# Stage 1 of a three-stage attention kernel: where the first group's leftover keys are multiplied, and as how many products

## The chip, the cores and the metric

The kernel runs on one core of a Trainium2 chip. The metric is the device time of one execution in microseconds (us); less is better. Beside the timed runs there is one profiled execution, whose trace all rows below come from. Engines are named as the profile names them: PE is TensorE (its weight loads stand apart as PEld), DVE is VectorE, ACT is ScalarE, POOL is GpSimd, and SP is SyncE, which issues most DMA transfers.

## The reference

Three layers follow each other: attention with rotary positions over 4 batches, 8 heads, 576 positions and 64 values a head; a gated feed-forward layer that mixes positions; and an attention layer with four experts. Only the first is touched. Cut to it:

```
def _attn_ref(q, k, v):
    ...
    q_rot, k_rot = (rotate(q), rotate(k))
    scale = 1.0 / np.sqrt(D)
    scores = scale * np.matmul(q_rot, k_rot.transpose(0, 1, 3, 2))
    scores = scores - np.max(scores, axis=-1, keepdims=True)
    attn = np.exp(scores)
    attn = attn / (np.sum(attn, axis=-1, keepdims=True) + 1e-09)
    return np.matmul(attn, v).astype(np.float32)
```

## The kernel before

Stage 1 is the attention layer. Its work comes in 16 units: one unit is a pair of heads of one batch. A unit has nine blocks of 128 query rows. Blocks 0, 2, 4, 6 hold queries of the first head and blocks 1, 3, 5, 7 of the second, 128 queries each; block 8 holds the last 64 queries of both heads. For each block the kernel makes the scores against the 576 keys in a PSUM tile `ps_S` (there are two, used in turn), the maximum of each row (`nmax`, on VectorE), the exponential (`e`, on ScalarE, straight from PSUM), and then transposes of `e` on TensorE (`ps_t`, four transposes of 128 keys each), which ScalarE or VectorE copies to SBUF (`g`). With the transposed exponentials as moving operand and the values `v` as weights TensorE makes the output, 64 rows for each head, in one PSUM tile `ps_o` of which there is only one.

576 keys are four times 128 and 64 left over. The leftover 64 keys of the two heads of a pair of blocks are put side by side by VectorE (`gather`), transposed together on TensorE (`ps_l`) and copied by ScalarE to `tl0` (first group) or `tl1` (second). The key rows 0 to 63 of `tl0` belong to the first head, 64 to 127 to the second. The weights for the leftover keys are kept as 128 rows by 2 x 64 columns, with zeros where key rows and output head don't belong together.

The output is made in two groups: the first group is the queries of blocks 0 to 3 (256 columns), the second those of blocks 4 to 8 (320 columns). `av(second, part)` issues the products of a group, and `out(second)` evicts `ps_o` with ScalarE (`xt`) and stores it through SyncE's queue.

A product for one head writes 64 of the 128 rows of `ps_o`, so it uses 64 columns of the array; the products of the two heads follow each other in column halves. The trace shows a plain f32 product as two records, so four products of one call stand as x8.

The order of instructions is written out by hand. The loop runs over slots k, of which each unit has nine, x = 0 to 8. Within slot x of a unit ScalarE makes the exponential of block x, TensorE the scores of block x + 1 (in slot 8: block 0 of the next unit) and the transposes of block x - 1, and VectorE the maximum of block x + 1. Around this regular work the other steps stand at given slots. For the unit whose slots these are, `av(False, 0)` stands at the end of slot 5, `av(False, 1)` at the end of slot 7 and `out(False)` in slot 8, behind the exponential. The second group follows in slots 1, 3 and 4 of the next unit (`av(True, 0)`, `av(True, 1)`, `out(True)`). Engines run their own instructions in this order; SyncE's queue is ordered by the recording layer.

Other work of stage 1 on the same engines: rotation of the next units' q and k on POOL and DVE, splitting of the weights `w_in` (`wt`, `raw`, `wih`; in most slots of odd units, in one of even units), and normalization of finished heads (`sa` times `sr`).

Of the kernel before, what the change touches and what calls it, by code (L numbers as in the profile page):

```python
# [40 lines left out]
def fused_kernel(ctx, tc, qk, v, w_in, w_out, w_sg, g_ln, b_sg, wqk, wvg, wo, rope, cst, out):  # L41
# [17 lines left out]
    PE, ACT, DVE, POOL = Engine(nc.tensor), Engine(nc.scalar), Engine(nc.vector), Engine(nc.gpsimd)  # L59
# [9 lines left out]
    def bank(t):  # L69
        shape = [P, 2, 512] if t.isupper() else [P, 512]  # L70
        return ps[t].tile(shape, F32, tag="b", name="ps_" + t)
# [271 lines left out]
    with ExitStack() as st:  # L343
# [19 lines left out]
        tl0 = ptp.tile([P, 256], F32, name="tl0")  # L363
# [10 lines left out]
        class Work:  # L374
# [110 lines left out]
            def av(self, second, part):  # L485


                if part == 0:
                    self.o = bank("o")
                n = 320 if second else 256  # L490
                for kb in ((0, 1), (2, 3, 4))[part]:
                    for j in range(2):
                        if kb < 4:
                            m = (g1 if second else g0)[:, kb, n * j:n * j + n]
                        else:
                            m = tl1[:, 64 * j:64 * j + 320] if second else tl0
                        PE.matmul(self.o[64 * j:64 * j + 64, 0:n], self.vt[:, kb, j, :], m, start=(kb == 0), stop=(kb == 4))
# [23 lines left out]
        def slot(k):  # L521


            n, x = divmod(k, 9)
            (nk, xk), (nn, xn) = divmod(k - 1, 9), divmod(k + 1, 9)
            w, p, wk, wn, nx = [works.get(i) for i in (n, n - 1, nk, nn, n + 1)]

            if w:
                w.exps(x)
            if x == 8 and w:  # L530
                w.out(False)
            if x == 4 and p:
                p.out(True)

            if wn:
                if xn == 0:
                    wn.start()
                wn.scores(xn)
            if wk:
                wk.turn(xk)  # L540
            for at, g, i in ((4, w, 0), (5, w, 1), (7, w, 2), (0, p, 3), (1, p, 4)):
                if x == at and g:
                    g.turn_left(i)
            if x == 1 and p:
                p.turn_factor()

            if wn:
                wn.maxima(xn)
            for at, g, i in ((1, w, 0), (3, w, 1), (5, w, 2), (7, w, 3), (0, p, 4)):
                if x == at and g:  # L550
                    g.gather(i)
            if x == 0 and p:
                p.factor(0)

            if n == 0 and x == 3:
                works[1].rope(1, (2,), DVE)
            if wk:
                wk.place(xk)
            if x == 0 and p:
                p.factor(1)  # L560
            if x == 2 and p:
                p.place_left(True)
                p.store_factor()
            if x == 5 and w:
                w.place_left(False)

            if x in (1, 3) and p:
                p.av(True, x // 2)
            if x in (5, 7) and w:
                w.av(False, x // 2 - 2)  # L570

            if nx:
                if x == (2 if n == 0 else 1):
                    nx.parts(0)
                if x == (4 if n == 0 else 3):
                    nx.parts(1)
                if n + 2 < B * NP:
                    if x == 3:
                        works[n + 2] = Work()
                        works[n + 2].load(n + 2)  # L580
                    if x == (7 if n == 0 else 4):
                        works[n + 2].rope(0)
                    if x == (8 if n == 0 else 7):
                        works[n + 2].rope(1)
                if x == 4 and n + 2 < B * NP:
                    works[n + 2].load_values()
# [30 lines left out]
        for k in range(9 * B * NP + 7):  # L617
            n, x = divmod(k, 9)
            slot(k)
            if x in ((1, 3, 4, 6, 7, 8) if n % 2 else (7,)):  # L620
                next(wload, None)
            if k == 9 * 4:
                steps = attended(bx, 0)
            if k == 9 * 14:
                lsteps = leftover(bx, 0)
            if n >= 4 and x == 8:
                next(steps, None)
            if n >= 14 and x == 3:
                next(lsteps, None)
            if k == 9 * 15 + 1:  # L630
                nsteps = attended(bx, 1)
            if k > 9 * 15 and x in (1, 5):
                next(nsteps, None)
# [37 lines left out]
    with ExitStack() as st:  # L671
# [210 lines left out]
        for b in range(1, B):  # L882
# [7 lines left out]
            if b == 2:  # L890
                w = wc.tile([P, 12, DM], F32R, tag="w", name="w")
# [28 lines left out]
    with ExitStack() as st:  # L920
# [436 lines left out]
        w, g = works[2 * B - 1], op[B - 1]  # L1357
# [102 lines left out]
```

## Time and profile before

| | |
|---|---|
| median of three timed runs | 708.77 us (706.46 to 709.38) |
| the profiled execution's own time | 709.53 us |
| its span, first to last instruction | 707.8 us |
| share of the span that PE, DVE, ACT, POOL count as busy | 96%, 65%, 61%, 49% |

The span is the trace's own measure; the time holds 1.7 us more, around it. A busy share is an average over three stages with different limits, and matmul ends are modelled. The rows that tell what sets the pace in stage 1 are in the section below.

### The profile page before, as it was taken

To read this page: it belongs to the slowest core of one execution; us is meant where nothing else is said; L and a number is where in the kernel's file an instruction comes from. 1 tells how busy PE (TensorE), PEld (TensorE's weight loads), DVE (VectorE), ACT (ScalarE), POOL (GpSimd) and SP (SyncE) were. 2 spreads that over 40 slices of the span, in tenths; PEclk is the share of its full clock that TensorE was granted. 3 is DMA by queue.
4 is the path that set the end of the run, shared out by engine and by line. 5 is a ranking of instruction groups with operands and counts; after the bars stand their busy time and mean duration, and the time that the engine had idled before them with its cause. 6 is when DMAs were issued, how large, how long until landed. Compare 5 with 4: busy or idle time off the path is not lost. (4 is left out here: it accounts for less than half of the span.)

```text
span 707.8 us, 13720 instructions
## 1 busy us (share of the span) xinstructions
PE 677.8 (96%) x4813; PEld 588.2 (83%) x4813; DVE 463.5 (65%) x1015; ACT 434.3 (61%) x1046; POOL 344.8 (49%) x321
## 2 busy tenths in 40 slices
PE   6899999999999999999999999999998999999996
PEld 6777677777776776798999899999998989999875
DVE  5786758686867676478874664664246666556674
ACT  6677776767677776565572473472055676666673
POOL 1886767676878770471545227216131453342320
PEclk9899999999999999999999999999998999999999
DMA  8668868778887864362365233054573354452521
GB/s 302 177 201 261 251 194 238 211 218 233 244 226 215 236 156 121 112 205 62 124 191 177 84 119 117 9 150 138 135 194 87 87 153 114 114 130 59 145 77 67
DMA packets 65286, 112.10 MB, mean 158 GB/s; under 512 B 20513, under 2 KB 25474, under 8 KB 65218
## 3 DMA queue, kind: packets, MB, share of 16 engines
q1 hardware_dynamic: 62482, 105.55, 51.7%
q10 hardware_dynamic: 2736, 5.68, 2.6%
q8 instruction: 38, 0.62, 0.4%
q14 instruction: 30, 0.25, 0.1%
HBM read 57.96 MB, written 18.98 MB: 109 GB/s over the span
## 5 line engine op out<-in xcount | busy, mean ns | idle before, releaser
L55 DVE TENSOR_REDUCE nmax<-ps_S 128x1 f32<-128x576 f32 x144 | 108.0, 750 | 71.9 <-PE ps_S L55 71.9
L55 ACT ACTIVATE e<-ps_S,nmax 128x576 f32<-128x576 f32 x144 | 107.0, 743 | 74.3 <-DVE nmax L55 70.3
L55 PE MATMUL ps_t<-ident,e 128*128 128x128 f32 x776 | 122.2, 275 | 4.6 <-ACT e L55 3.6
L55 PEld LDWEIGHTS ps_t<-ident,e 128*128 128x128 f32 x776 | 95.4, 141 | 10.2 <-ACT e L55 5.2
L55 PE MATMUL ps_S<-kh,q 128*128 128x288 f32 x352 | 86.0, 337 | 13.8 <-ACT e L55 10.9
L55 POOL TENSOR_TENSOR t<-t,rp 128x576 f32<-128x576 f32 x61 | 89.5, 1487 | 15.0 <-ACT rp L55 9.2
L55 PEld LDWEIGHTS ps_S<-kh,q 128*128 128x128 f32 x352 | 52.9, 191 | 47.2 <-ACT e L55 29.6
L55 PE MATMUL ps_o<-g,v 128*64 128x320 f32 (+1 forms) x512 | 76.2, 419 | 0.0
L55 POOL TENSOR_TENSOR lo<-t,hi 128x576 fp32r<-128x576 f32 x30 | 42.8, 1428 | 56.0 <-DVE hi L55 56.0
L55 PE MATMUL ps_S<-lo,qz 128*128 128x288 f32 x304 | 66.2, 300 | 1.5 <-DVE lo L55 1.5
L55 PE MATMUL ps_S<-yh,w 128*128 128x288 f32 x256 | 52.9, 310 | 0.9 <-DVE nmax L55 0.9
L55 PEld LDWEIGHTS ps_o<-g,v 128*64 128x64 f32 x512 | 31.4, 136 | 24.1 <-issue 8.9
L55 PEld LDWEIGHTS ps_S<-lo,qz 128*128 128x128 f32 x304 | 49.6, 192 | 1.7 <-DVE lo L55 1.7
L55 ACT ACTIVATE e<-e,nmax 128x128 f32<-128x128 f32 (+4 forms) x72 | 42.2, 585 | 14.0 <-DVE nmax L55 13.8
L55 POOL TENSOR_TENSOR yl<-x,yh 128x640 fp32r<-128x640 f32 x16 | 26.0, 1628 | 47.4 <-ACT yh L55 45.7
L55 ACT COPY g<-ps_t 128x512 f32<-128x512 f32 x80 | 46.3, 579 | 2.3 <-PE ps_t L55 1.3
L55 POOL TENSOR_TENSOR t<-t 128x576 f32<-128x576 f32 x29 | 43.6, 1502 | 2.3
L55 DVE COPY g<-ps_t 128x512 f32<-128x512 f32 x64 | 43.5, 680 | 0.5 <-PE ps_t L55 0.5
L55 PEld LDWEIGHTS ps_S<-yh,w 128*128 128x128 f32 x256 | 39.9, 194 | 1.3 <-DVE nmax L55 1.3
L55 ACT ACTIVATE ga<-ga 128x512 f32<-128x512 f32 (+1 forms) x34 | 22.3, 656 | 26.7 <-DVE ga L55 26.7
L55 PE MATMUL ps_S<-wsh,vh 128*128 128x288 f32 x160 | 34.6, 298 | 0.8 <-DVE u L55 0.5
L55 POOL TENSOR_TENSOR gxl<-u,gxh 128x576 fp32r<-128x576 f32 x16 | 22.8, 1432 | 23.9 <-ACT gxh L55 23.9
(281 smaller groups left out, 1782.3 us busy)
## 6 DMA issues: line engine op xcount, KB each, us to landing
t<-in_qk_dram SPq DMA_DIRECT2D x32, 576.0 KB
kh<-hi SPq DMA_DIRECT2D x92, 144.0 KB
q<-hi SPq DMA_DIRECT2D x38, 144.0 KB
qz<-hi SPq DMA_DIRECT2D x38, 144.0 KB
q<-lo SPq DMA_DIRECT2D x38, 144.0 KB
v<-in_v_dram SPq DMA_DIRECT2D x16, 320.0 KB
sa<-xr SPq DMA_DIRECT2D x16, 288.0 KB
xd<-sa SPq DMA_DIRECT2D x16, 288.0 KB
```

Of the source, the lines that this page charges most:

```text
L55: ins = op(*a, **k)
```

## The change

The leftover keys of the first group are no longer multiplied for each head in a column half, at the end of `av(False, 1)` in slot 7. They become one product over all 128 columns of the array, a third part of `av`, at the end of slot 8. The zeros in the weights make it the sum that the two products made. `out(False)` follows it: it moves from slot 8 to slot 0 of the next unit, and stands there for the unit before (`p`).

```
-                for kb in ((0, 1), (2, 3, 4))[part]:
+                if part == 2:
+                    PE.matmul(self.o[:, 0:n], self.vt[:, 4].rearrange("p j d -> p (j d)"), tl0, start=False, stop=True)
+                    return
+                for kb in ((0, 1), (2, 3, 4) if second else (2, 3))[part]:
...
             if w:
                 w.exps(x)
-            if x == 8 and w:
-                w.out(False)
+            if x == 0 and p:
+                p.out(False)
             if x == 4 and p:
                 p.out(True)
...
-            if x in (5, 7) and w:
-                w.av(False, x // 2 - 2)
+            if x in (5, 7, 8) and w:
+                w.av(False, {5: 0, 7: 1, 8: 2}[x])
```

TensorE's order from slot 7 of unit 4 to slot 0 of unit 5, before:

```order
L55 MATMUL ps_o<-g_194,v 64x256 x4
L55 MATMUL ps_o<-tl_196,v 64x256 x2
L55 MATMUL ps_S<-kh,q_1_172 128x288 x2
L55 MATMUL ps_S<-lo_1244,qz_173 128x288 x2
L55 MATMUL ps_t<-ident,e 128x128 x4
L55 MATMUL ps_S<-kh,q_1_172 128x288 x2
L55 MATMUL ps_S<-lo_1244,qz_173 128x288 x2
L55 MATMUL ps_t<-ident,e 128x128 x4
L55 MATMUL ps_l<-ident,e 128x128
```

The same stretch of TensorE with the change:

```order
L55 MATMUL ps_o<-g_194,v 64x256 x4
L55 MATMUL ps_S<-kh,q_1_172 128x288 x2
L55 MATMUL ps_S<-lo_1240,qz_173 128x288 x2
L55 MATMUL ps_t<-ident,e 128x128 x4
L55 MATMUL ps_o<-tl_196,v 128x256
L55 MATMUL ps_S<-kh,q_1_172 128x288 x2
L55 MATMUL ps_S<-lo_1240,qz_173 128x288 x2
L55 MATMUL ps_t<-ident,e 128x128 x4
L55 MATMUL ps_l<-ident,e 128x128
```

The two products of 64 rows ahead of the score of the next unit's block 0 are gone, and one of 128 rows stands behind that score and the transposes of block 7, ahead of the score of block 1.

ScalarE's order from the exponential of block 8 of unit 4 on, before:

```order
L55 ACTIVATE e,sums<-ps_S,nmax 128x576
L55 COPY xt<-ps_o 128x256
L55 ACTIVATE e,sums<-ps_S,nmax 128x576
L55 ACTIVATE rs<-sums 128x9
L55 COPY g_195<-ps_t 128x4x2x64
L55 ACTIVATE e,sums<-ps_S,nmax 128x576
L55 COPY g_194<-ps_t 128x4x128
L55 ACTIVATE wt<-raw 128x512
L55 ACTIVATE e,sums<-ps_S,nmax 128x576
```

The same stretch of ScalarE with the change:

```order
L55 ACTIVATE e,sums<-ps_S,nmax 128x576 x2
L55 COPY xt<-ps_o 128x256
L55 ACTIVATE rs<-sums 128x9
L55 COPY g_195<-ps_t 128x4x2x64
L55 ACTIVATE e,sums<-ps_S,nmax 128x576
L55 COPY g_194<-ps_t 128x4x128
L55 ACTIVATE wt<-raw 128x512
L55 ACTIVATE e,sums<-ps_S,nmax 128x576
```

The eviction `xt` now stands behind the exponential of the next unit's block 0 instead of ahead of it.

SyncE's queue around the border from unit 5 to unit 6, before (`xr` is the store of the first group, `sr` the loads for the normalization, `q_1` and `qz` the fills for the unit after):

```order
L506 DMA xr_64<-xt 128x256
L229 DMA raw<-in_w_in_dram 128x1024
L300 DMA xd_0_71<-sa 128x576
L198 DMA sr<-rd_67 64x576
L199 DMA sr<-rd_67 64x64
L200 DMA sr<-rd_67 64x512
L166 DMA q_1_172<-hi_1636 64x576
```

The same place of SyncE's queue with the change:

```order
L229 DMA raw<-in_w_in_dram 128x1024
L509 DMA xr_64<-xt 128x256
L300 DMA xd_0_71<-sa 128x576
L198 DMA sr<-rd_67 64x576
L199 DMA sr<-rd_67 64x64
L166 DMA q_1_172<-hi_1630 64x576
```

The store moved behind the load of `raw`, and the third load of `sr` moved to the end of that unit's transfers, ahead of the next unit's store.

## Rows read from the trace of the kernel before

**Rows 1.** The page, part 1: busy time, share of the span, instructions.

```profile
PE 677.8 (96%) x4813; PEld 588.2 (83%) x4813; DVE 463.5 (65%) x1015; ACT 434.3 (61%) x1046; POOL 344.8 (49%) x321
```

**Rows 2.** PE's waits, 13.9 to 287 us: total, times, longest.

```profile
PE ps_S L55 <- ACT e L55: 10.9, 24, 1.6
```

**Rows 3.** Timeline of PE, units 4 and 5: start, length, instruction, count, [idle before].

```profile
98.48 1.08 PE L55 MATMUL ps_o<-g,v 128*64 128x256 f32 x8
...
99.92 0.53 PE L55 MATMUL ps_S<-kh,q 128*128 128x288 f32 x2
...
101.52 0.60 PE L55 MATMUL ps_t<-ident,e 128*128 128x128 f32 x4
101.95 0.27 PE L55 MATMUL ps_l<-ident,e 128*128 128x128 f32 x1
102.43 0.53 PE L55 MATMUL ps_S<-kh,q 128*128 128x288 f32 x2 [0.20 <-ACT e L55]
...
106.02 0.51 PE L55 MATMUL ps_S<-kh,q 128*128 128x288 f32 x2
```

**Rows 4.** Timeline of DVE, the same stretch: maxima of blocks 0 and 1.

```profile
100.75 0.76 DVE L55 TENSOR_REDUCE nmax<-ps_S 128x1 f32<-128x576 f32 x1 [1.80 <-PE ps_S L55]
...
102.03 0.75 DVE L55 TENSOR_REDUCE nmax<-ps_S 128x1 f32<-128x576 f32 x1
```

**Rows 5.** Timeline of ACT, the same stretch.

```profile
100.04 0.37 ACT L55 COPY xt<-ps_o 128x256 f32<-128x256 f32 x1 [0.25 <-PE ps_o L55]
101.55 0.74 ACT L55 ACTIVATE e<-ps_S,nmax 128x576 f32<-128x576 f32 x1 [1.13 <-DVE nmax L55]
...
102.38 0.58 ACT L55 COPY g<-ps_t 128x512 f32<-128x512 f32 x1
102.84 0.75 ACT L55 ACTIVATE e<-ps_S,nmax 128x576 f32<-128x576 f32 x1
...
104.18 0.69 ACT L55 ACTIVATE wt<-raw 128x512 f32<-128x512 f32 x1
104.78 0.72 ACT L55 ACTIVATE e<-ps_S,nmax 128x576 f32<-128x576 f32 x1
```

**Rows 6.** Timeline of PE, end of slot 5 of unit 5.

```profile
111.29 1.08 PE L55 MATMUL ps_o<-g,v 128*64 128x256 f32 x8
112.30 0.53 PE L55 MATMUL ps_S<-kh,q 128*128 128x288 f32 x2
```

**Rows 7.** Stretches of the warm-up, instructions on `ps_l` alone: stretch, busy (count), clock.

```profile
4.32:4.98 0.66, 0.66 (x8) 0.66 (x7) 0.00 (x0) 1.00 1.01 419
4.32:6.10 1.78, 1.78 (x18) 1.78 (x17) 0.00 (x0) 1.00 1.01 412
```

**Rows 8.** The page, part 5: full-array weight loads, total and mean ns.

```profile
L55 PEld LDWEIGHTS ps_S<-kh,q 128*128 128x128 f32 x352 | 52.9, 191 | 47.2 <-ACT e L55 29.6
```

**Rows 9.** Timeline of all engines, border of units 5 and 6.

```profile
114.41 1.95 DVE L55 SCALAR_TENSOR_TENSOR wt<-raw,wt 128x512 int32<-128x512 int32 x1
...
116.28 0.74 DVE L55 TENSOR_REDUCE nmax<-ps_S 128x1 f32<-128x576 f32 x1
...
117.12 0.74 ACT L55 ACTIVATE e<-ps_S,nmax 128x576 f32<-128x576 f32 x1 [1.73 <-DVE nmax L55]
...
118.00 0.54 PE L55 MATMUL ps_S<-kh,q 128*128 128x288 f32 x2 [0.52 <-ACT e L55]
```

**Rows 10.** Timeline of ACT, unit 4: the exponential of block 3.

```profile
90.34 0.74 ACT L55 ACTIVATE e<-ps_S,nmax 128x576 f32<-128x576 f32 x1 [1.15 <-DVE nmax L55]
```

**Rows 11.** Tile `sa` (min/median/max ns), and the timeline at border 14-15.

```profile
L55 DVE TENSOR_TENSOR sa<-sa,sr x4: 741/743/1893, 119.4 to 271.3; 128x576 f32<-128x576 f32 x4
...
271.14 1.41 POOL L55 TENSOR_TENSOR sa<-sa,sr 128x576 f32<-128x576 f32 x1 [7.05 <-DMA sr<-rd]
...
274.02 0.33 PE L55 MATMUL ps_l<-ident,e 128*128 128x128 f32 x1 [1.10 <-DVE e L55]
```

**Rows 12.** A stretch in stage 3: busy by engine, clock (0.50), DMA.

```profile
535.00:540.00 5.00, 4.84 (x21) 4.84 (x22) 2.13 (x10) 2.21 (x7) 0.22 (x1) 0.50 0.25 66
```

## Prediction

> **What bounds the kernel now.** I read the page's busy times first: TensorE counts as busy for 96% of the span [rows 1]. So the question is where it still waits. The view of the waits, cut to the first stage, answers it: its score products stood still for 10.9 us in 24 waits, each for the exponentials `e` on ScalarE [rows 2]. There are two S buffers, so the score of block x+2 takes the buffer of block x once the exponential of block x has read it. The loop is: score, maximum on VectorE, exponential on ScalarE, score two blocks on. Where the timeline of TensorE shows a wait, this loop (or what holds VectorE up in it) sets the pace; where it shows none, TensorE's own work does.
>
> The timeline around one border between units, from unit 4 to unit 5, shows both. In slot 7 of unit 4 the values products and the leftover pair run from 98.48 to the score of the next unit's block 0 at 99.92. TensorE then works without a wait until the score of block 2, which stands at 102.43 and waited 0.20 us for `e` [rows 3]. VectorE sat idle for 1.80 us before the maximum of that block 0, until its score came [rows 4], and ScalarE for 1.13 us before its exponential [rows 5]. So here the loop begins with the score at 99.92, and that score stands behind the leftover pair on TensorE.
>
> **The change, part by part.** *What it removes.* In slot 5 TensorE needs 1.01 us from the first values product (four of them, eight records, since a plain f32 product stands in the trace as two) to the next score; those are 111.29 and 112.30 [rows 6]. In slot 7 it needs 99.92 - 98.48 = 1.44 us with the leftover pair behind the same four [rows 3]. The pair costs 0.43 us; the change of array shape before the score is paid in both slots and stays.
>
> *What it adds.* One full-array f32 product of 256 columns, two records. The trace has such products only in the warm-up, with 128 columns: ten more of their records take 1.78 - 0.66 = 1.12 us at full granted clock [rows 7], 0.112 us each. Two records with twice the columns are 4 x 0.112 = 0.45 us. The bound below is the 0.43 us of the pair itself. So TensorE saves nothing: -0.43 + 0.45 = +0.02 us a unit. Whatever comes of the change comes of the place.
>
> *Weight loads against the array.* A full-array load of weights takes 191 ns [rows 8], yet in the warm-up the loads and products advance together at 0.112 us a record [rows 7], so loads run under products of the same shape. The Trainium skill, "TensorE: Matmul & The Clock Gate", Part 3 (The mechanism), states the contrary for a case like this: a load overlaps with running products only where its row group is another one. By that rule the new product, behind full-array transposes, would pay its two loads openly. This trace does not agree in the warm-up. What open loads would do here is priced under the rivals.
>
> *Even unit to odd unit (borders 0-1, 2-3, ..., 12-13: seven).* The score of block 0 comes at 99.92 - 0.43 = 99.49. The maximum and the exponential follow it, as both engines were idle, and the eviction at 100.04 [rows 5] no longer stands ahead: the exponential goes from 101.55 to 101.12 and ends at 101.12 + 0.74 = 101.86. Before, it ended at 102.29 and the score of block 2 began 0.14 later; now it may begin at 102.00. TensorE itself is free after the one leftover transpose, at 101.95 + 0.11 (its neighbours start (101.95 - 101.52) / 4 = 0.11 apart) + 0.02 = 102.08 [rows 3]. So the wait of rows 3 goes, and the score of block 2 begins about 0.35 earlier, 0.45 with its open weight load.
>
> What is late next? ScalarE. The exponential of block 1 starts behind its maximum, which ends at 102.03 + 0.75 = 102.78 [rows 4]; that score stands behind the new product in slot 8, so it does not come earlier (-0.43 + 0.45). From 102.84 ScalarE works without a pause through the copy of the transposes and the weights' `wt` at 104.18 to the exponential of block 2, 104.78 to 105.50 [rows 5]. The score of block 4 needs its buffer and cannot begin before 105.50 + 0.14 = 105.64; it began at 106.02 [rows 3]. That is 0.38 us at most; a score that waited has its loads open (0.53 against 0.51 us in rows 3), so I take 0.36. After that ScalarE has gaps again and TensorE leads. Seven borders give 2.52 us; bounds 0 and 7 x 0.45.
>
> *The eviction in slot 0.* `xt<-ps_o` costs 0.37 us [rows 5], and behind it stand `rs`, the copy of the transposes at 102.38 and the exponential of block 1. The exponential of block 0 ends 0.43 earlier at these borders, so the copy comes at 102.38 - 0.43 + 0.37 = 102.32 and the exponential of block 1 could start at 102.78: still 0.06 inside what VectorE allows. It is covered, narrowly. The next product into the `o` bank comes only in slot 1, at the first second-group values product, over a microsecond behind it.
>
> *Odd unit to even unit (seven).* Here VectorE is the one that is late: a weights' operation of 1.95 us starts at 114.41, the maximum of block 8 follows at 116.28, its exponential at 117.12 after ScalarE waited 1.73, and TensorE's score of block 1 waits 0.52 for that [rows 9]. An earlier score of block 0 changes nothing in this chain. The new product lies in that wait, which grows to 0.52 + 0.43: hidden, worth 0; without that cover it would cost 0.45. The eviction now stands ahead of the exponentials of blocks 1 and 2 and may push them by 0.37; ScalarE idles 1.15 us before the exponential of block 3 [rows 10], so this is swallowed. Price if it weren't: 0.37.
>
> *Border 14-15.* VectorE's product `sa` takes 1.89 us there, where others take 0.74 [rows 11], and TensorE waits 1.10 for `e` behind it; a product on GpSimd runs beside it from 271.14. The chain still begins with the score of block 0, so 0.43 us is gained. If `sa` gets ahead of GpSimd, up to 1.15 more; I take none.
>
> *SyncE.* The first group's store moves one slot on with its eviction; the next unit's fills of q come more than a slot behind it. Some loads of `sr` move past fills, but are read a whole unit later: 0. The last unit's border gives nothing, since its transposes of block 8 wait for an exponential anyway.
>
> **Sum.** 2.52 + 0.43 = 2.95 us from the profiled execution's 709.53: 706.6. That execution lay 0.76 over the median of the three timed runs, 708.77; from the median it is **705.8 us**. The later stages keep TensorE fed and move as a whole. The low clock after the wait near 533 us (0.50 granted in the stretch 535 to 540 [rows 12]) I take as unchanged.
>
> **The rivals.**
> 1. *More than forecast.* The seven borders give 0.45 and `sa` at border 14-15 gets free of GpSimd: 8 x 0.45 + 1.15 = 4.75, 704.0. For it: only ScalarE's unbroken run holds the 0.45 back. Against it: that run is there in each odd unit.
> 2. *Nothing comes of it.* The wait of 0.20 goes and returns at once: ScalarE's run from 102.84 is the pace of slots 0 to 3, and the score of block 4 doesn't move. Then 708.8. Against it: 0.38 us of slack in rows 3 and 5.
> 3. *Open weight loads.* With two loads of 0.19 open, the product is 0.83 us; at eight borders 0.38 of the gain is lost, and 0.0 to 0.05 stays: 708.4 to 708.8. Against it: rows 7. (This is what the rule of the skill named above would give.)
> 4. *Slower: the eviction on the path.* If the exponential of block 1 starts behind the eviction by all of 0.37 and every odd and even unit's next scores wait for it, 16 x 0.37 = 5.9 is lost and the gain with it: 714.7. It decides when ScalarE's 0.06 inside VectorE's time is gone and the 0.38 before the score of block 4 too. Against it: the 1.15 idle of rows 10, the earlier exponential of rows 5.
>
> **How the numbers follow.** About 0.5% (3.5 us) is what a measurement of this kernel tells from no change, and the forecast lies just inside. Chances: the forecast 0.55 (705.0 to 707.0), rival 1 0.17, rival 2 0.14, rival 3 0.07, rival 4 0.07. Under 705.2 lie rival 1 and a small part of the forecast's own spread: faster 0.30; slower 0.07, rival 4; same 0.63. The range leaves out rival 4 and the far ends: 703.6 to 709.2. It takes in the bounds 0 (708.8) and most of 4.75.
>
> **What the profile after would show.** Slot 7 with eight `ps_o` records and a score about 1.01 us behind the first; in slot 8 two `ps_o<-tl` records of 128*128 behind the transposes, the next score 0.45 us later than now. At even-odd borders the eviction behind the exponential of block 0; no wait of 0.20 before the score of block 2, a small one before that of block 4, and 6.17 us between the scores of blocks 0 and 4 (99.92 to 106.02 now, 6.10), begun 0.43 earlier. At odd-even borders the same times as now, relative to the border. It is wrong if the exponential of block 1 starts later than the end of its maximum at even-odd borders, if the new product takes 0.8 us, or if the score of block 4 stays where it was relative to the unit's slot 6.

## The result, and the profile after

The kernel with the change takes **699.25 us** (median of 4 runs, 698.72 to 700.3); the kernel before took 708.27 on the same chip (4 runs, 706.46 to 709.38). The ratio is 0.9877, with a 95% interval of 0.9851 to 0.9902: 9.0 us faster, where 2.95 were forecast. The range (703.6 to 709.2) did not hold it.

The profiled execution took 699.69 us with a span of 697.9, against 709.53 and 707.8. I followed the start of every score product through stage 1 in both traces. At the last one the trace after is 8.9 us ahead, and this is where it got ahead (an even-odd border is one from an even unit to an odd one):

| place | gain of each, us | together |
|---|---|---|
| even-odd borders 0-1 to 12-13 (seven) | 0.42 to 0.45 | 3.05 |
| odd-even borders 1-2, 7-8 and 11-12 | 1.25 to 1.28 | 3.78 |
| the other four odd-even borders | 0.0 | 0 |
| border 14-15 | 1.59 | 1.59 |
| start of the stage, ahead of the first changed instruction | 0.5 | 0.5 |

The last 1.0 us of the span lies in the later stages. They took 423.9 us in the trace before and 422.9 after, and 421.4 to 423.8 in the ten traces below, so I count that as scatter. So I do the 0.5 us ahead of the first changed instruction: at that place the ten traces lie between 0.5 us later and 0.8 us earlier than the trace before.

**The even-odd border.** The page, part 1, after: busy time, share, instructions; it answers to [rows 1].

```profile
PE 675.7 (97%) x4781; PEld 590.3 (85%) x4781; DVE 459.8 (66%) x1015; ACT 432.6 (62%) x1046; POOL 345.8 (50%) x321
```

PE's waits after, from 13.9 us to the end of stage 1; it answers to [rows 2].

```profile
PE ps_S L55 <- ACT e L55: 5.9, 11, 1.0
```

Timeline of PE after, units 4 and 5: start, length, instruction, count. It answers to [rows 3].

```profile
95.80 1.08 PE L55 MATMUL ps_o<-g,v 128*64 128x256 f32 x8
96.82 0.53 PE L55 MATMUL ps_S<-kh,q 128*128 128x288 f32 x2
97.19 0.43 PE L55 MATMUL ps_S<-lo,qz 128*128 128x288 f32 x2
97.45 0.60 PE L55 MATMUL ps_t<-ident,e 128*128 128x128 f32 x4
97.89 0.60 PE L55 MATMUL ps_o<-tl,v 128*128 128x256 f32 x2
98.13 0.61 PE L55 MATMUL ps_S<-kh,q 128*128 128x288 f32 x2
98.58 0.43 PE L55 MATMUL ps_S<-lo,qz 128*128 128x288 f32 x2
98.85 0.60 PE L55 MATMUL ps_t<-ident,e 128*128 128x128 f32 x4
...
99.33 0.53 PE L55 MATMUL ps_S<-kh,q 128*128 128x288 f32 x2
...
102.92 0.51 PE L55 MATMUL ps_S<-kh,q 128*128 128x288 f32 x2
```

TensorE's waits for the exponentials fell from 24 (10.9 us) to 11 (5.9 us). Slot 7 is as forecast: the score of block 0 stands 96.82 - 95.80 = 1.02 us behind the first values product, where it was 1.44. In slot 8 the new product is two records. The load of weights for the second of them ran beside the first (the records start 0.22 us apart, a load takes 0.19). The score of block 2 (99.33) no longer waits, that of block 4 (102.92) doesn't either, and from block 0 to block 4 it is 6.10 us, exactly as before. So TensorE now paces this stretch throughout, and the whole of it begins 0.43 earlier.

Timelines of DVE and ACT after, the same border; they answer to [rows 4, 5].

```profile
97.65 0.76 DVE L55 TENSOR_REDUCE nmax<-ps_S 128x1 f32<-128x576 f32 x1 [1.37 <-PE ps_S L55]
98.32 0.68 DVE L55 COPY g<-ps_t 128x512 f32<-128x512 f32 x1
99.05 0.76 DVE L55 TENSOR_REDUCE nmax<-ps_S 128x1 f32<-128x576 f32 x1
```

```profile
98.44 0.74 ACT L55 ACTIVATE e<-ps_S,nmax 128x576 f32<-128x576 f32 x1 [1.32 <-DVE nmax L55]
...
99.18 0.36 ACT L55 COPY xt<-ps_o 128x256 f32<-128x256 f32 x1
...
100.01 0.76 ACT L55 ACTIVATE e<-ps_S,nmax 128x576 f32<-128x576 f32 x1
...
101.20 0.71 ACT L55 ACTIVATE wt<-raw 128x512 f32<-128x512 f32 x1
101.79 0.76 ACT L55 ACTIVATE e<-ps_S,nmax 128x576 f32<-128x576 f32 x1
```

This slot began at 95.80, before at 98.48; add 2.68 to compare with the rows of before. The maximum of block 1 stands at 101.73 against 102.03, the exponential of block 1 at 102.69 against 102.84, that of block 2 at 104.47 against 104.78. So the maximum and the exponential of block 1 came earlier, though the score that they read didn't: its second half stands at 98.58 + 2.68 = 101.26, and before it stood at 101.25 in the timeline of PE:

```profile
101.25 0.43 PE L55 MATMUL ps_S<-lo,qz 128*128 128x288 f32 x2
```

**The odd-even border**, where nothing was expected. Timeline of DVE and of POOL after, border 1-2 and then border 3-4.

```profile
46.11 0.68 DVE L55 SCALAR_TENSOR_TENSOR wt<-raw,wt 128x512 int32<-128x512 int32 x1
46.71 0.75 DVE L55 TENSOR_REDUCE nmax<-ps_S 128x1 f32<-128x576 f32 x1
...
78.08 1.95 DVE L55 SCALAR_TENSOR_TENSOR wt<-raw,wt 128x512 int32<-128x512 int32 x1
79.95 0.74 DVE L55 TENSOR_REDUCE nmax<-ps_S 128x1 f32<-128x576 f32 x1
```

```profile
46.12 3.79 POOL L55 TENSOR_TENSOR t<-t,rp 128x576 f32<-128x576 f32 x2
...
78.07 3.23 POOL L55 TENSOR_TENSOR t<-t,rp 128x576 f32<-128x576 f32 x2
```

One and the same weights' operation takes 0.68 us at border 1-2 and 1.95 at border 3-4, the length that it has in [rows 9]; the maximum behind it moves with it. Beside it GpSimd starts its rotation products, within 0.01 us of it both times. Where VectorE's operation is short, GpSimd's two products take 3.79 us instead of 3.23. So they keep each other out; that whoever is first is served whole is what experiments 2 to 4 test. The trace before had the short length too: in the last unit, where GpSimd has no product beside it, its timeline of DVE shows

```profile
285.00 0.69 DVE L55 SCALAR_TENSOR_TENSOR wt<-raw,wt 128x512 int32<-128x512 int32 x1
```

The two meet at every odd-even border because they start from one place: GpSimd's product `lo` waits for VectorE's cast `hi`, and three more products follow it up to the contested one. VectorE reaches the weights' operation 5.87 to 5.88 us behind the start of `lo` at all seven borders in both traces. At border 1-2 after, `lo` stands in the timeline of POOL as

```profile
40.25 1.46 POOL L55 TENSOR_TENSOR lo<-t,hi 128x576 fp32r<-128x576 f32 x1 [1.17 <-DVE hi L55]
```

Over the seven operations of slot 6 the trace after has three short ones (borders 1-2, 7-8, 11-12: the three that gained) and four of 1.95; the trace before has seven of 1.93 to 1.95.

The same shows at border 14-15. Tile `sa` after (min/median/max ns), which answers to [rows 11]:

```profile
L55 DVE TENSOR_TENSOR sa<-sa,sr x4: 740/741/747, 116.3 to 263.5; 128x576 f32<-128x576 f32 x4
```

The product that took 1.89 us takes 0.75, as it now starts 1.1 us ahead of GpSimd's instead of 0.14 behind it (GpSimd's stood at 271.14, [rows 11]). Timelines, DVE before, then DVE and POOL after:

```profile
271.28 1.89 DVE L55 TENSOR_TENSOR sa<-sa,sr 128x576 f32<-128x576 f32 x1
...
263.53 0.75 DVE L55 TENSOR_TENSOR sa<-sa,sr 128x576 f32<-128x576 f32 x1
...
264.60 1.41 POOL L55 TENSOR_TENSOR sa<-sa,sr 128x576 f32<-128x576 f32 x1 [7.78 <-DMA sr<-rd]
```

The clock is no part of it. The low stretch in stage 3 is there as before [rows 12]; it begins 8 us earlier, after the shorter stage 1, and lasts 6.8 us in both traces:

```profile
525.00:530.00 5.00, 3.69 (x17) 3.54 (x16) 3.10 (x10) 1.84 (x6) 0.58 (x2) 0.51 0.24 66
```

### The profile page after: what moved, and what is told of

It reads as the page before. It is cut to its first block, busy times and chain, and to the rows that moved or that the text cites. A ratio compares the mean times of both kernels' runs of the same rounds, so it can differ in the third digit from the quotient of the medians.

```text
span 697.9 us, 13660 instructions
## 1 busy us (share of the span) xinstructions
PE 675.7 (97%) x4781; PEld 590.3 (85%) x4781; DVE 459.8 (66%) x1015; ACT 432.6 (62%) x1046; POOL 345.8 (50%) x321
## 4 chain that ended last, share of the span: by engine, by line
PE 82%; DVE 9%; ACT 4%; DMA 2%; issue 2%; SPq 1%; POOL 0%; ACTq 0%; POOLq 0%; DVEq 0%
PE ps_S L55 45%; PE ps_o L55 16%; PE ps_t L55 13%; PE ps_f L55 4%; PE ps_s L55 3%; DVE wt L55 2%; PE ps_l L55 1%; DVE nmax L55 1%; ACT e L55 1%; ACT qz L55 1%; DVE e L55 1%; DVE ga L55 1%; DMA ws<-in_w_sg_dram 1%; DMA t<-in_qk_dram 1%; DVE h1l L55 0%
## 5 line engine op out<-in xcount | busy, mean ns | idle before, releaser
L55 POOL TENSOR_TENSOR t<-t,rp 128x576 f32<-128x576 f32 x61 | 91.2, 1518 | 14.5 <-ACT rp L55 9.2
```

The source lines that it names most:

```text
L55: ins = op(*a, **k)
```

## The experiments

In the expectations, theory A is that a tie between VectorE's weights' operation in slot 6 of the odd units and GpSimd's rotation product decides 1.25 us at each odd-even border; theory B is that the operation is short where the change took work away. Ratios are to the kernel before on the same chip, with the 95% interval.

**1. Both kernels again, unchanged.** The kernel before:

> The kernel before, unchanged, for a second trace. Theory A (the long gain at three odd-even borders is a tie between VectorE's weights' operation and GpSimd's rotation, which start within 0.03 us of each other): the timed runs spread over 706.5 to 709.4 and the seven borders may fall either way, most of them with the operation at 1.95 us, 0 to 2 of them at 0.68. Theory B (the operation is short because the change took work away at that border): all seven at 1.93 to 1.95 us.

706.02 us (10 runs, 702.71 to 709.41), ratio 0.9995 (0.9975 to 1.0015). Its profiled run was the longest of the ten. Tile `raw` of its trace in stage 1, where the weights' operation of slot 6 stands with another of 1.1 us, seven each:

```profile
L55 DVE SCALAR_TENSOR_TENSOR wt<-raw,wt x14: 1107/1522/1946, 47.3 to 252.9; 128x512 int32<-128x512 int32 x14
```

No operation is short: all seven of slot 6 are at 1.93 to 1.95. Both theories allowed that, so this run doesn't tell between them. The kernel with the change:

> The changed kernel again, for a second trace and more times. Theory A: three to five of the seven borders fall to the short operation in most executions, but not always the same ones; times from 696 to 703 in steps of about 1.26 us. Rival: the same three borders (1-2, 7-8, 11-12) in each trace and times within 1 us, so that the outcome belongs to the program.

700.11 us (6 runs), ratio 0.9909 (0.9881 to 0.9937). The even-odd borders are 0.42 to 0.47 shorter again and 14-15 by 1.59. Of the odd-even borders only 1-2 (1.28) and 7-8 (1.25) are; 11-12, short in the first trace, is not. The same program falls one way or the other there, as a tie would. Neither expectation came whole: two borders are short, not three to five and not the same three, and the six times lie within 2.1 us (698.7 to 700.9), not in steps from 696 to 703.

**2. GpSimd held back a little, without the change.**

```
+        nap = one.tile([P, 1], F32, name="nap")
...
                     if x == (8 if n == 0 else 7):
+                        if n % 2:
+                            POOL.memset(nap, 0.0)
                         works[n + 2].rope(1)
```

> The kernel before, with a write of one column on GpSimd ahead of its second rotation in the seven odd units up to 13, so that GpSimd comes to the tie later. Theory A: VectorE's operation takes 0.68 us at all seven borders, 7 x 1.26 = 8.8 us less: 699.5. Theory B: nothing but the write is added, 708.3, the operation stays at 1.93 to 1.95 us.

703.91 us (12 runs, 701.75 to 705.61), ratio 0.9967 (0.9948 to 0.9985); 699.5 was expected. The mechanism came, its size didn't. All seven operations take 0.68 us, but the borders 1-2, 3-4 and 13-14 gain only 0.98 to 1.01, 11-12 gains 1.26, and 5-6, 7-8 and 9-10 lose 0.17 to 0.21. Timelines of DVE and of PE, border 3-4, and then DVE at border 5-6 and POOL there:

```profile
79.77 0.68 DVE L55 SCALAR_TENSOR_TENSOR wt<-raw,wt 128x512 int32<-128x512 int32 x1
...
82.45 0.76 DVE L55 TENSOR_REDUCE nmax<-ps_S 128x1 f32<-128x576 f32 x1 [0.18 <-PE ps_S L55]
...
116.38 1.93 DVE L55 TENSOR_TENSOR sa<-sa,sr 128x576 f32<-128x576 f32 x1
```

```profile
81.08 0.60 PE L55 MATMUL ps_o<-tl,v 128*64 128x256 f32 x4
81.61 0.53 PE L55 MATMUL ps_S<-kh,q 128*128 128x288 f32 x2
```

```profile
116.28 1.42 POOL L55 TENSOR_TENSOR t<-t 128x576 f32<-128x576 f32 x1
```

With VectorE early, the maximum of block 0 waits 0.18 us for its score, and that stands behind the leftover pair (81.08): the pair that the change takes away. (At 11-12 the exponential of block 0 is queued behind two casts on ScalarE and starts without a wait, so an earlier score would not help there.) And where `sa` follows in the same unit, VectorE now reaches it 0.10 us behind a GpSimd product and pays 1.93 us there.

**3. The same with the change.**

> The changed kernel with the same write on GpSimd. Theory A: the four borders that kept the long operation lose it too, 4 x 1.26 = 5.0 us: 694.2. Theory B: 699.3.

694.44 us (5 runs, 693.0 to 695.96), ratio 0.9834 (0.9807 to 0.9861). The same kernel on another chip:

> The changed kernel with a memset of one column on GpSimd ahead of its rotation product in seven odd units, unchanged from its first run. Theory A: VectorE is first at all seven, all seven operations take 0.68 us, all odd-even borders are 1.25 us shorter than before: 694.4 us again, 8.6 under the kernel with the memset on VectorE (7 x 1.25 = 8.75). Theory B: as the changed kernel, 699 to 700.

694.35 us (5 runs, 692.0 to 695.11), ratio 0.9789 (0.9767 to 0.9811). In both traces all seven odd-even borders gain 1.23 to 1.28, the even-odd borders 0.40 to 0.44, and 14-15 gains 1.56 to 1.58. This version beats the kernel before on both chips, and lies some 5 us under the one with the change (699.25 and 700.11 against 694.44 and 694.35; the two were not timed side by side; the four ties that it lost are 4 x 1.25 = 5.0).

**4. VectorE held back instead, with the change.**

```
+            if x == 6 and n % 2 and n + 2 < B * NP:
+                DVE.memset(nap, 0.0)
             if x in ((1, 3, 4, 6, 7, 8) if n % 2 else (7,)):
```

> The changed kernel, with a memset of one column on VectorE ahead of the weights' operation of slot 6 in seven odd units. Theory A (a tie between VectorE's weights' operation and GpSimd's rotation product decides 1.25 us at each odd-even border): GpSimd is now first at all seven, so all seven operations take 1.93 to 1.95 us, no odd-even border is shorter than before, the even-odd borders keep their 0.43; the three short borders of the changed kernel are lost: 699.3 + 3 x 1.26 = 703.0 us, 702.5 to 704. Theory B (the odd-even gain comes from the new product's place, and the tie only goes with it): the borders 1-2, 7-8 and 11-12 stay shorter by over 1 us, and the time stays at 699 to 700.

703.24 us (6 runs, 700.88 to 704.33), ratio 0.9918 (0.9899 to 0.9937), on the same chip as the second run of 3. Tile `raw` in stage 1, of this kernel and then of the one in 3:

```profile
L55 DVE SCALAR_TENSOR_TENSOR wt<-raw,wt x14: 1096/1518/1950, 46.9 to 249.9; 128x512 int32<-128x512 int32 x14
```

```profile
L55 DVE SCALAR_TENSOR_TENSOR wt<-raw,wt x14: 680/894/1115, 46.9 to 241.1; 128x512 int32<-128x512 int32 x14
```

With VectorE late, none of 14 is under 1.10 us, and the seven of slot 6 are at 1.94 to 1.95; with GpSimd late, none is over 1.12. With VectorE late every odd-even border is within 0.02 of before; the even-odd ones keep their 0.41 to 0.45 and 14-15 its 1.58. Both kernels do the same work on TensorE, and their times differ by 8.9 us; 7 x 1.25 = 8.75. Theory B (the new product's place gives the odd-even gain) has fallen. It also divides the result: with no tie won, the change gives 5.4 us on this chip.

**5. Which half of the change?** Two column halves, but in slot 8:

```
-                    PE.matmul(self.o[:, 0:n], self.vt[:, 4].rearrange("p j d -> p (j d)"), tl0, start=False, stop=True)
+                    for j in range(2):
+                        PE.matmul(self.o[64 * j:64 * j + 64, 0:n], self.vt[:, 4, j, :], tl0, start=False, stop=True)
```

> The changed kernel, but with the leftover keys as two products in column halves, in slot 8. If the place alone made the gain at the even-odd borders: 699.3 but for ties, and the score of block 2 there stands 0.43 us earlier than before. If the one product matters too, since column halves behind full-array transposes pay for the change of the array's shape on both sides (0.1 to 0.2 us each by the gaps around the values products): some 0.3 us at each of eight even-odd borders comes back, 701.7, and the score of block 2 there gains only about 0.1.

705.84 us (12 runs), ratio 0.9978 (0.9958 to 0.9999); 701.7 was expected if the form matters, counting the ties that the changed kernel won, but here none of the seven was won. One product, but in slot 7 as before (eviction in slot 8):

```
+                        if kb < 4 or second:
                             PE.matmul(self.o[64 * j:64 * j + 64, 0:n], self.vt[:, kb, j, :], m, start=(kb == 0), stop=(kb == 4))
+                        elif j == 0:
+                            PE.matmul(self.o[:, 0:n], self.vt[:, 4].rearrange("p j d -> p (j d)"), tl0, start=False, stop=True)
```

> The kernel before with the form alone changed: one product over the whole array, still in slot 7, eviction still in slot 8. If the gain at the even-odd borders is the place alone: the score of block 2 stands where it stands before, within 0.05 us, and the time is that of before, 706 to 708. If the one product is itself cheaper than the pair: the score of block 0 comes earlier by more than 0.1 us at each border.

704.08 us (10 runs), ratio 0.9977 (0.9956 to 0.9999); 706 to 708 was expected. Timelines of PE, unit 4's slots 7 and 8, first of the pair in slot 8, then of the one product in slot 7:

```profile
99.66 0.43 PE L55 MATMUL ps_S<-lo,qz 128*128 128x288 f32 x2
...
100.45 0.65 PE L55 MATMUL ps_o<-tl,v 128*64 128x256 f32 x4
...
101.39 0.43 PE L55 MATMUL ps_S<-lo,qz 128*128 128x288 f32 x2
```

```profile
97.66 1.08 PE L55 MATMUL ps_o<-g,v 128*64 128x256 f32 x8
98.67 0.70 PE L55 MATMUL ps_o<-tl,v 128*128 128x256 f32 x2
...
99.47 0.43 PE L55 MATMUL ps_S<-lo,qz 128*128 128x288 f32 x2
...
101.61 0.53 PE L55 MATMUL ps_S<-kh,q 128*128 128x288 f32 x2 [0.20 <-ACT e L55]
```

From the second half of one score (`lo`) to that of the next, slot 8 takes 101.39 - 99.66 = 1.73 us with the pair and 98.58 - 97.19 = 1.39 in the kernel with the change. Between full-array products the one is 0.34 us cheaper. The pair has the array change between 128 and 64 columns ahead of it and behind it; that this is the reason is argued, no run isolates it. The even-odd borders with the pair in slot 8 gain 0.10 to 0.14 only, and of its 2.2 us in stage 1 1.44 are `sa` at 14-15, where VectorE was first (0.75 us; GpSimd's took 1.89). In slot 7 the one product gains nothing: no border moves by more than 0.05, and the wait of 0.20 is back. So neither half is enough: the place takes 0.43 off the path, the form keeps 0.34 of it from being paid again. The 0.2% of the one product in slot 7 lies outside its borders: its trace is 0.8 us ahead by block 6 of the first unit, which its edit doesn't reach, and has the shortest later stages of all (421.4 us). A difference of that size between two programs is not explained by any of this.

**6. The eviction alone.** `out(False)` in slot 0 of the next unit, products as before:

```
-            if x == 8 and w:
-                w.out(False)
+            if x == 0 and p:
+                p.out(False)
```

> The kernel before with the eviction alone moved to slot 0. Theory A: ScalarE's 0.37 us ahead of the exponential of block 1 uses up slack at the even-odd borders, so 0 to 0.1 us is lost at each, up to 0.8 in all, and the odd-even borders with a long weights' operation do not change: 707 to 708. If the gain were the eviction's: 703 to 704.

706.76 us (10 runs), ratio 0.9999 (0.9977 to 1.0022); no border moves by more than 0.09. Timeline of ACT, border 4-5:

```profile
101.75 0.74 ACT L55 ACTIVATE e<-ps_S,nmax 128x576 f32<-128x576 f32 x1 [1.76 <-DVE nmax L55]
...
102.48 0.36 ACT L55 COPY xt<-ps_o 128x256 f32<-128x256 f32 x1
...
103.31 0.76 ACT L55 ACTIVATE e<-ps_S,nmax 128x576 f32<-128x576 f32 x1
```

The exponential of block 1 follows that of block 0 by 1.56 us, where it was 1.29 [rows 5]: the eviction does push it, by 0.27, and nothing comes of it. With the memset of experiment 2 as well:

> The kernel before with the write on GpSimd and the eviction in slot 0, the leftover pair still in slot 7. The odd-even borders gave 1.0 us with the write alone and 1.26 with the write and the whole change. If the 0.26 between them is ScalarE's eviction standing ahead of the weights' cast: 1.26 here too. If it is the leftover pair standing ahead of the score of block 0 on TensorE: 1.0 here, and 703 to 704 in all.

704.53 us (10 runs), ratio 0.9972 (0.9955 to 0.999), border by border as in experiment 2, with the same wait of 0.18 for the score at border 3-4; 703 to 704 was expected. So it was the leftover pair, not the eviction, that kept 0.26 there. 14-15 gained 1.15 besides, with `sa` at 0.75 us.

## Why the prediction was wrong

The direction was forecast as less likely than no change (0.30 against 0.63), and the size at a third.

**Odd-even borders, forecast 0, measured 3.8 in three: the step that failed.** It reads: "An earlier score of block 0 changes nothing in this chain." That is so while the weights' operation takes 1.95 us: at the four borders that kept it the score of block 0 does come 0.43 earlier, and that of block 1 stands where it stood. The step that failed is to take 1.95 us as the operation's price. It is a price with 1.27 us of waiting in it. The same operation takes 0.68 or 0.69 us where GpSimd is idle (276.09 after, 285.00 before). Experiments 2 to 4 show it: a memset of one column decides all seven borders, for VectorE in each of four traces with it on GpSimd, for GpSimd in the one with it on VectorE. The Trainium skill, "SBUF — State Buffer", section "SBUF: two separate sides", states that VectorE and GpSimd share a port pair as an exclusive lock, which an operation of VectorE with two inputs in SBUF and one of GpSimd that reads SBUF both need: whichever starts first gets it for the whole instruction, and the other blocks. These traces agree: 0.68 against 1.95 us on VectorE (`wt<-raw,wt` has two such inputs), 3.79 against 3.23 on GpSimd. That the Trainium skill has such a rule and [rows 11] the same clash at `sa` should have led me to ask for the shortest and longest of every VectorE operation beside GpSimd. The change does tip the ties: in the five traces without the whole change and without a memset (the kernel before twice, experiment 5's two, the eviction alone) GpSimd won all 35; in the two with it VectorE won 5 of 14. Which part of the change does it isn't settled: the two starts lie some 0.01 us apart in the records, finer than they tell the order (with the pair in slot 8 GpSimd's is level or 0.001 us behind at four borders, and VectorE still took 1.96 us), and border 11-12 fell differently in two traces of the same program. So the gain here is not mere chance, but nothing that I knew would have told how many of the seven the change wins. But where a tie is won, the change is worth more than the tie alone, 1.25 instead of 1.00, since the score of block 0 no longer stands behind the pair (experiments 2 and 6).

**Border 14-15, forecast 0.43, measured 1.59.** "If `sa` gets ahead of GpSimd, up to 1.15 more; I take none": it got ahead, and gave 1.16 (1.59 - 0.43). The mechanism was seen, the choice was wrong. It came in all five traces with the new product in slot 8, and in those of experiments 5 (pair in slot 8) and 6 (eviction and memset) too; it did not come with the eviction alone, the memset alone or the one product in slot 7. GpSimd's product there starts when its load of `sr` lands ([rows 11]: it waited 7.05 us for it), so this is a race between a transfer and VectorE. Its margin can be read from the traces: counted from the score of block 5 of unit 14, VectorE reaches `sa` after 9.41 or 9.42 us in the six traces with the leftover keys in slot 7 and after 8.98 to 9.02 in the six with them in slot 8; GpSimd starts after 9.13 to 10.33. Before, VectorE was late by 0.14 us, less than the 0.43 that the change gives it, so the forecast's own 0.43 spoke for the win, unless the load landed earlier too. What moves the landing of `sr` from trace to trace I didn't isolate; with eviction and memset it alone decided (10.33).

**Even-odd borders, forecast 0.36, measured 0.42 to 0.45.** The mechanism was right. The limit of 0.38 was not there, because "that score stands behind the new product in slot 8, so it does not come earlier" is true of the score, and I took it for the maximum. In [rows 4] the maximum of block 1 shows no wait for its score: it was queued behind the maximum of block 0 and the copy of the transposes on VectorE, and came 0.30 earlier with them. ScalarE's run moved 0.31, and the score of block 4 the full 0.43. This I read from the two traces; no run tested it by itself. The 0.02 us that I took off for open weight loads (0.53 against 0.51 us "a score that waited") has no ground either: the score at 99.92 shows 0.53 without a wait [rows 3]. Over seven borders both come to 0.5 us.

**What held.** The pair costs 0.43 (1.44 - 1.02 = 0.42). The new product costs 0.43 at its border (from 96.82 to the transposes at 98.85, 2.03 us, where it was 101.52 - 99.92 = 1.60), forecast 0.45; TensorE indeed saves nothing there, and the gain is the place. The eviction is covered: the exponential of block 1 starts 0.20 us behind its maximum's end at 99.81, which I had named as a sign of failure, but it is still earlier than before, and experiment 6 prices the eviction at nothing. SyncE's new order did nothing that I could find, unless the landing of `sr` at border 14-15 is its doing, which no run separates.

**The rivals.** Rival 1 (704.0) came whole, 0.43 a border and `sa` free, and 699.25 is still 4.8 under it, 3.8 of that the tie. Rival 2 fell, the score of block 4 moved. Rival 3 fell: the new product cost 0.43 and not the 0.83 that two open weight loads make. The sentence of the Trainium skill that the prediction named beside it ("TensorE: Matmul & The Clock Gate", Part 3 (The mechanism)) did not hold in this place. The same section also lets a load run ahead into a background weight buffer, which the prediction left out; with that case the measured 0.43 agrees. Rival 4 fell with experiment 6.

## What to carry to other kernels

When one operation has two lengths in a trace, ask what ran beside it before taking the longer one as its price: here 1.27 of 1.95 us was waiting for GpSimd's instruction, and a memset of one column, placed so that VectorE is first, was worth some 5 us on top of the change. A chain that waits for one engine's queue moves with that queue, so "its input comes no earlier" is an argument only where the row shows a wait for that input. To move a product is only a gain if its form fits its new neighbours: between full-array products two column halves cost 0.34 us more than one whole product, while behind other column halves (slot 7) the one gained nothing.

## What the runs showed of the hardware

A tie within some 0.01 us between VectorE and GpSimd fell either way in two traces of the same program (border 11-12), at 1.25 us each time, and an edit that touches neither of the two operations took VectorE from 0 of 35 such ties to 5 of 14. So a comparison of two versions can hold several won or lost ties that have nothing to do with what the edit was for; the length of the contested operation in each trace shows how many. The kernel before spread from 702.7 to 709.4 us over ten runs, and its profiled run, with all seven ties lost, was the longest; the changed one with all ties set by a memset spread over 3.0 to 3.5 us, and with the ties left open over 1.6 and 2.1. So the spread doesn't tell how many ties a run won, and whether the runs without a profile win some isn't shown.
